# One weight load of a window-attention decode kernel, issued from ScalarE's DMA queue instead of SP's

## The chip, the cores and the metric

The kernel runs on one core of a Trainium2 chip. A core has a matrix engine (TensorE, PE in the profile), a vector engine (VectorE, DVE), an activation engine (ScalarE, ACT), a general engine (GpSimd, POOL) and a synchronization engine (SyncE, SP) that here only issues transfers. Each engine works through its own list of instructions in order and waits on semaphores that other engines or transfers raise. Transfers between device memory and the on-chip memory (128 partitions) run on 16 DMA engines. They are issued by an engine's instruction into that engine's queue: in the profile q1 is the queue of SP, q10 that of ScalarE.

The metric is the device time of one execution in microseconds, lower is better, as the median over runs. The profile is of one execution; its span is a little shorter than that execution's time.

## The reference, cut to what matters

```python
xn = layernorm(x)                                   # x: 2 x 1 x 512
# attention over the last W = 4096 of 32768 cached positions; 32 query heads, 8 kv heads, 128 wide
q = (xn @ wq).reshape(B, 1, 32, 128).transpose(0, 2, 1, 3)
k, v = (repeat(c[:, :, Sk - W:, :], 4, axis=1) for c in (k_cache, v_cache))
p = softmax(einsum("bhqd,bhkd->bhqk", q, k) * 128 ** -0.5)
s = einsum("bhqk,bhkd->bhqd", p, v).transpose(0, 2, 1, 3).reshape(B, 1, 4096) @ wo
# gated unit on the same xn; Fh = 896
z = gelu(xn @ w_in)                                 # w_in: 512 x 1792
z1, z2 = z[..., :Fh], layernorm(z[..., Fh:])
g = w_sp * z2 + b_sp                                # w_sp is 1 x 1, b_sp has one element
out = x + s * silu((z1 * g) @ w_out)                # w_out: 896 x 512
```

Everything is float32. For two rows of x the kernel reads 89.4 MB of weights and cache.

## The kernel before, in words

**The ring.** All large loads go into `ring` (line 80): four slots of 4 MB, 32 KB in each of the 128 partitions. `enqueue` (line 85) gives each load the next slot or slots in turn; `advance` (line 92) marks slots as free and issues whatever loads at the head of the list have all of theirs. The turn is fixed: w_in in slot 0 (3.5 MB), w_out in slot 1 (1.75 MB), wq in slots 2 and 3 (8 MB); then, for eight units (a unit is one batch row and two kv heads), k and v tiles of 4 MB in the order k0, k1, v0, k2, v1, k3 and so on, and last wo in seven pieces. The first three loads find their slots free and are issued at once, at lines 120 to 122; a later one is issued when its slot's last reader is done: k0 after the `z` matmuls (`advance(0)`), k1 after the `y` matmuls (`advance(1)`), v0 and k2 after the `q_ps` matmuls (`advance(2, 3)`), and from there a k tile's slot passes on after its last transpose, a v tile's after its `acc` matmuls. All these loads are issued by SP, in that order: a load that waits for its slot keeps those behind it waiting too.

**Order.** The engines TensorE, VectorE, ScalarE and SP are wrapped in `InOrder` (line 27), which keeps each one's instructions in the order of the program. Since its `issue` (line 37) emits them all, most rows of the profile name line 37; the tiles tell them apart.

**ScalarE's queue.** ScalarE issues three small loads: `xs` (x, 4 KB, line 109), then the two scalars of the gate, `w_sp` and `b_sp`, into `wb1` (lines 126 and 127; the profile calls the tile wb). Between line 109 and line 126 stand the three `enqueue` calls.

**The stages.** Layernorm of x gives `xnT`. TensorE computes `z` (xn @ w_in), and right behind it, as its next instruction, `wb_ps`, a small matmul that spreads the two scalars over the partitions:

```python
    advance(0)
    wb_ps = bank("wb_ps", "mo")[:, :2]
    pe.matmul(wb_ps, ones[0:1, :], wb1, start=True, stop=True)
    wb = const("wb", 2)
    dve.tensor_copy(wb, wb_ps)
    zs = const("zs", 2 * FQ)
    act.activation(zs, pz, AF.Copy)
```

On VectorE the copy into `wb` is followed by the transpose of `zs`, the gelu, the two means (matmuls `mean_ps` and `var_ps`) and `hT`. TensorE then does `y` (hT with w_out) and `yq`; VectorE and ScalarE make the sigmoid gate of it, which is used only at the very end. After `yq` TensorE does `q_ps` (xn @ wq); VectorE arranges q in `qbd`. Then the units follow: VectorE transposes each k tile in four pieces (`kt`, four a unit), TensorE multiplies (`sh`, `s`), softmax runs on VectorE and ScalarE, and TensorE applies v (`acc`) one unit behind. Last come the `part` and `so` matmuls with wo, the gate, the addition of x and the store.

Of the kernel before, what the change touches and what calls it, by code (L numbers as in the profile page):

```python
# [14 lines left out]
P = 128  # L15
# [27 lines left out]
def kernel(  # L43
# [14 lines left out]
    pe, dve, act, sp = (InOrder(tc, e) for e in (nc.tensor, nc.vector, nc.scalar, nc.sync))  # L58
# [7 lines left out]
    FT = FH // P  # L66
# [15 lines left out]
    queue = []  # L82
    turns = [0]

    def enqueue(load, count=1):

        at = turns[0] % 4
        turns[0] += count
        queue.append((load, range(at, at + count)))
        advance()  # L90

    def advance(*slots):
        for n in slots:
            free[n] = True
        while queue and all(free[n] for n in queue[0][1]):
            load, at = queue.pop(0)
            for n in at:
                free[n] = False
            load(ring[:, at[0] * SLOT : (at[-1] + 1) * SLOT], at[0])
# [9 lines left out]
    act.dma_start(xs, x[:, 0, :])  # L109
    weight = {}  # L110

    def load_rows(name, w, k):
        def load(t, at):
            n = k * w.shape[1]
            sp.dma_start(t[:, :n], w.rearrange("(p k) f -> p (k f)", p=P))
            weight[name] = t[:, :n].rearrange("p (k f) -> p k f", k=k)

        return load

    enqueue(load_rows("in", w_in, KT))  # L120
    enqueue(load_rows("out", w_out, FT))
    enqueue(load_rows("q", wq, KT), 2)
    win, wout, wqt = (weight[n] for n in ("in", "out", "q"))

# [391 lines left out]
    for n in range(EARLY):  # L516
        t, a = blocks[n]
# [5 lines left out]
    for n in range(EARLY, 32):  # L523
        if n == LATE:
            spread_quarters(so, parts, start=False, stop=False)
        t, a = blocks[n]
# [37 lines left out]
```

## Time and profile before

| what | value |
|---|---|
| median of 3 runs | 217.91 us (217.8 to 218.05) |
| the profiled execution's own time | 217.37 us |
| its span | 215.6 us |
| TensorE busy | 156.5 us, 73% |
| VectorE busy | 107.5 us, 50% |
| ScalarE busy | 44.0 us, 20% |
| large loads, on q1 | 89.40 MB, 97.0% of 16 DMA engines' time |
| granted TensorE clock, mean | 0.849 |

How to read the rows that follow. In a timeline a row is start, duration, engine, line, operation, output<-input, count, and in brackets the idle time before it and what ended that. In the chain that ended last, a row is start, duration and what the time went to. A row of the stages has the stage, its length, busy time and instructions of the five engines, the granted TensorE clock, the mean busy share of the DMA engines and GB/s. A DMA queue's row has packets, MB and the time of those packets as a share of 16 engines; packets are counted in the window in which they begin, so that a narrow window can show more than 100%. A DMA issue's row has the size and the time from issue to landing. A row of the waits has who waited for whom: us in total, times, longest.

### The profile page before, as it was taken

How to read it: one execution, taken by the hardware profiler on the slowest of the kernel's cores; microseconds unless marked ns; L12 is line 12 of the kernel's file. 1: busy time of each engine (PE TensorE's matmuls, PEld its weight loads, DVE VectorE, ACT ScalarE, POOL GpSimd, SP SyncE). 2: the span in 40 equal slices, each digit the busy share in tenths (PEclk: the TensorE clock that was granted, in tenths of full speed). 3: DMA queues.
4: the chain of work that ended last, by engine and by line, in shares of the span. 5: the costliest groups of instructions: out<-in, count | busy, mean ns of one | idle time of the engine just before them, and what ended most of it. 6: DMA issues, size and time to landing. Idle time of an engine off the chain costs nothing.

```text
span 215.6 us, 2230 instructions
## 1 busy us (share of the span) xinstructions
PE 156.5 (73%) x866; PEld 43.6 (20%) x866; DVE 107.5 (50%) x168; ACT 44.0 (20%) x109; POOL 3.9 (2%) x21
## 2 busy tenths in 40 slices
PE   0164273952994995995997699559959948999793
PEld 0121110210121221221221222222212212222321
DVE  3304313058968647837906941695587089240101
ACT  5002410000223143133113304120431421232001
POOL 6100000000000000000000000000000000000000
PEclk9999567695598899799699679958997995899799
DMA  7999898999999999999999999999999999999991
GB/s 251 426 528 401 389 499 371 423 444 409 456 407 450 426 435 432 426 438 413 450 412 438 432 438 435 432 432 407 432 444 423 444 426 450 413 441 413 404 388 40
DMA packets 3789, 89.54 MB, mean 415 GB/s; under 512 B 434, under 2 KB 450, under 8 KB 964
## 3 DMA queue, kind: packets, MB, share of 16 engines
q1 hardware_dynamic: 3772, 89.40, 97.0%
q8 instruction: 7, 0.11, 0.2%
q14 instruction: 2, 0.02, 0.0%
q10 hardware_dynamic: 8, 0.00, 0.0%
HBM read 89.40 MB, written 0.00 MB: 415 GB/s over the span
## 4 chain that ended last, share of the span: by engine, by line
DMA 48%; PE 34%; DVE 15%; issue 1%; SPq 0%; DVEq 0%
DMA ring<-in_A_wo_dram 20%; DMA ring<-in_A_wq_dram 16%; DMA ring<-in_A_k_cache_dram 12%; DVE kt L37 10%; PE s L37 10%; PE sh L37 9%; PE acc L37 7%; PE q_ps L37 4%; PE col L37 1%; PE mo L37 1%; DVE qm L37 1%; DVE qbd L37 1%; DVE m L37 1%; PE rp L37 1%; PE oT L37 0%
## 5 line engine op out<-in xcount | busy, mean ns | idle before, releaser
L37 DVE STREAM_TRANSPOSE kt<-ring 128x2048 f32<-128x2048 f32 x32 | 72.6, 2294 | 32.5 <-DMA ring<-in_A_k_cache_dram 30.5
L37 PE MATMUL sh<-kt,qbd 128*32 128x512 f32 x256 | 43.4, 727 | 14.0 <-DVE kt L37 14.0
L37 ACT ACTIVATE shs<-sh 128x512 f32<-128x512 f32 x32 | 19.1, 597 | 119.1 <-PE sh L37 119.1
L37 PE MATMUL s<-shs,add_dq 128*128 128x512 f32 x64 | 41.0, 748 | 0.0
L37 PE MATMUL acc<-ring,pT 128*32 128x512 f32 x256 | 30.3, 612 | 0.2 <-DVE pT L37 0.2
L37 PEld LDWEIGHTS s<-shs,add_dq 128*128 128x128 f32 x64 | 11.2, 219 | 31.1 <-issue 26.7
L37 PEld LDWEIGHTS sh<-kt,qbd 128*32 128x32 f32 x256 | 6.7, 114 | 34.2 <-issue 20.4
L37 PEld LDWEIGHTS acc<-ring,pT 128*32 128x32 f32 x256 | 7.4, 114 | 24.7 <-issue 15.5
L37 PE MATMUL q_ps<-ring,xnT 128*32 128x512 f32 x64 | 9.6, 770 | 3.6 <-DMA ring<-in_A_wq_dram 3.6
L37 PE MATMUL mo<-l,same_r 128*128 128x2 f32 x16 | 3.7, 299 | 10.7 <-ACT p L37 10.7
L37 DVE TENSOR_REDUCE m<-s 128x2 f32<-128x512 f32 x8 | 5.4, 675 | 9.1 <-PE s L37 9.1
L37 ACT ACTIVATE o<-acc,wd 128x128 f32<-128x128 f32 x32 | 9.1, 373 | 3.4 <-PE acc L37 3.4
L37 PE MATMUL z<-ring,xnT 128*32 128x448 f32 x32 | 5.6, 875 | 5.3 <-DMA ring<-in_B_w_in_dram 5.3
L37 ACT ACTIVATE p<-s,nb 128x256 f32<-128x256 f32 x16 | 7.6, 490 | 7.0 <-DVE nb L37 6.8
L37 PE MATMUL part<-ring,oT 128*32 128x512 f32 x56 | 7.9, 714 | 1.1 <-DMA ring<-in_A_wo_dram 1.1
L37 PE MATMUL col<-o,sel 128*32 128x512 f32 x16 | 8.3, 601 | 0.4 <-ACT o L37 0.4
L37 DVE STREAM_TRANSPOSE qT<-q_ps 128x512 f32<-128x512 f32 x2 | 1.4, 717 | 10.4 <-PE q_ps L37 10.2
L37 PE MATMUL y<-ring,hT 128*32 128x512 f32 x14 | 3.5, 1043 | 3.8 <-DVE hT L37 3.8
L37 DVE STREAM_TRANSPOSE pT<-p 128x512 f32<-128x512 f32 x8 | 5.4, 674 | 1.2 <-ACT p L37 1.2
L37 DVE TENSOR_TENSOR res<-so,gate 128x128 f32<-128x128 f32 x1 | 0.3, 292 | 10.8 <-PE so L37 10.8
L37 ACT ACT_TABLE_LOAD x4 | 5.1, 1283 | 1.9 <-issue 1.9
L37 PEld LDWEIGHTS mo<-l,same_r 128*128 128x128 f32 x16 | 3.0, 233 | 12.2 <-ACT p L37 12.2
(106 smaller groups left out, 63.2 us busy)
## 6 DMA issues: line engine op xcount, KB each, us to landing
ring<-in_A_k_cache_dram SPq DMA_DIRECT2D x8, 4096.0 KB, 27.5
ring<-in_A_v_cache_dram SPq DMA_DIRECT2D x8, 4096.0 KB, 30.1
ring<-in_A_wo_dram SPq DMA_DIRECT2D x1, 4096.0 KB, 34.2
ring<-in_B_w_in_dram SPq DMA_DIRECT2D x1, 3584.0 KB, 11.7
ring<-in_A_wo_dram SPq DMA_DIRECT2D x1, 2048.0 KB, 27.5
ring<-in_B_w_out_dram SPq DMA_DIRECT2D x1, 1792.0 KB, 15.5
ring<-in_A_wo_dram SPq DMA_DIRECT2D x1, 1024.0 KB
ring<-in_A_wo_dram SPq DMA_DIRECT2D x4, 256.0 KB, 16.7
```

The source lines that it names most:

```text
L37: return self.tc.keep_in_program_order(call(*args, **kwargs))
```

## The change

The helper that builds the loads of w_in, w_out and wq takes the issuing engine as an argument, SP unless another is given; for w_out ScalarE is given. The slots, the sizes, the access patterns and the order of the `enqueue` calls stay. In ScalarE's program the load stands where the `enqueue` call stands: behind `xs`, ahead of `w_sp` and `b_sp`. SP goes from w_in straight to wq.

```diff
-    def load_rows(name, w, k):
+    def load_rows(name, w, k, queue=sp):
         def load(t, at):
             n = k * w.shape[1]
-            sp.dma_start(t[:, :n], w.rearrange("(p k) f -> p (k f)", p=P))
+            queue.dma_start(t[:, :n], w.rearrange("(p k) f -> p (k f)", p=P))
             weight[name] = t[:, :n].rearrange("p (k f) -> p k f", k=k)
 
         return load
 
     enqueue(load_rows("in", w_in, KT))
-    enqueue(load_rows("out", w_out, FT))
+    enqueue(load_rows("out", w_out, FT, act))
     enqueue(load_rows("q", wq, KT), 2)
```

## The prediction

> **What bounds the kernel now.** I read the page first: busy shares, the slices, the DMA queues.
>
> ```profile
> span 215.6 us, 2230 instructions
> ...
> DMA  7999898999999999999999999999999999999991
> ...
> q1 hardware_dynamic: 3772, 89.40, 97.0%
> q8 instruction: 7, 0.11, 0.2%
> ...
> q10 hardware_dynamic: 8, 0.00, 0.0%
> ```
>
> q1 is SP's queue, with every large load; q10 is ScalarE's, with eight tiny packets. q1 keeps the 16 DMA engines busy for 97% of the span. To see whether that stream ever breaks I asked for busy time by stage, for VectorE's waits, and for the chain that ended last.
>
> ```profile
> 10.00:36.00 26.00, 11.08 (x60) 3.61 (x60) 6.66 (x26) 4.65 (x8) 0.00 (x0) 0.77 1.01 437
> 36.00:212.00 176.00, 144.46 (x798) 39.39 (x802) 96.45 (x122) 36.42 (x97) 0.00 (x0) 0.85 0.99 425
> ...
> DVE kt L37 <- DMA ring<-in_A_k_cache_dram: 30.5, 5, 7.4
> ...
> 1.65 34.42 DMA ring<-in_A_wq_dram
> 36.11 9.70 PE q_ps L37 x64
> ...
> 201.94 9.95 DMA ring<-in_A_wo_dram
> ```
>
> The last columns are the DMA share and GB/s: 1.01 and 0.99 from 10 to 212 us. Between those, compute alternates with the stream, and five times VectorE sits waiting for a k tile, up to 7.4 us. So the end is set by 89 MB through a queue that must not run dry, plus the 4 us around it. Moving a transfer within the stream costs nothing by itself; a load issued after the stream has caught up with it costs the whole gap. The question is what the change does to the issue times of the k and v loads.
>
> **The change, part by part.** The issues as they stand, from the timelines of SP and ScalarE (start, duration):
>
> ```profile
> 0.73 0.40 SPq L37 DMA_DIRECT2D ring<-in_B_w_in_dram  x1
> 1.20 0.41 SPq L37 DMA_DIRECT2D ring<-in_B_w_out_dram  x1
> 1.65 0.46 SPq L37 DMA_DIRECT2D ring<-in_A_wq_dram  x1
> ...
> 0.73 0.54 ACTq L37 DMA_DIRECT2D xs<-in_A_x_dram  x1
> 1.31 0.23 ACTq L37 DMA_DIRECT2D wb<-in_B_w_sp_dram  x1
> 1.57 0.27 ACTq L37 DMA_DIRECT2D wb<-in_B_b_sp_dram  x1
> ```
>
> SP loses one issue of 0.41 us, so wq is issued at 1.20 instead of 1.65; it stands behind w_in's rows either way, worth 0. ScalarE gains an issue of 0.41 us at 1.31, between xs and the two scalars, which go out at about 1.7 and 2.0; xs stays ahead of them all, and the layernorm behind xs ends well before w_in lands, so this too is 0. The count of DMAs does not change.
>
> What does change is the order on the DMA engines. How the engines share two queues is visible from q10's packets, found by asking for the DMA traffic in narrow windows: 0 to 2.5 us; 2.5 to 5.7; 5.8 to 5.9; 7.3 to 8.3; 9.0 to 9.1; then 17 to 34 us for wq.
>
> ```profile
> q10 hardware_dynamic: 4, 0.00, 1.3%
> ...
> q1 hardware_dynamic: 36, 1.03, 76.2%
> ...
> q10 hardware_dynamic: 1, 0.00, 0.6%
> ...
> q1 hardware_dynamic: 16, 0.46, 106.2%
> q10 hardware_dynamic: 1, 0.00, 0.1%
> ...
> q10 hardware_dynamic: 1, 0.00, 0.6%
> ...
> q1 hardware_dynamic: 112, 7.34, 99.6%
> ```
>
> The first four are xs and its completion marks. Then q10 moves nothing until 5.85 us, although w_sp was issued at 1.31; and the last of the scalars' four packets (w_sp, its mark, b_sp, its mark) comes at 9.05, the others one per us between. A w_in row (28 KB) takes 1.06 us: sixteen in one us on sixteen engines at 106%. So 4 packets of 4 bytes spanned three w_in rows: the engine gives each queue one packet in turn, and a mark is a packet. Of wq, 112 packets in 17 us at 99.6% of 16 engines make 64 KB and 2.42 us each. Each engine holds eight rows of each load; a w_out row is half a w_in row, 0.53 us (estimate from its bytes), a k or v row half a wq row, 1.21.
>
> The Trainium skill, "DMA: Bandwidth & Descriptors", section "Queues, rings and completion order", says that each engine goes round its queues packet by packet, and that a packet often holds 9 to 17 descriptors. The first half agrees with the four packets above; by the second, w_out's eight rows would pass in one turn, which is the second rival.
>
> Step 1: w_in. w_out now takes the place that w_sp had in ScalarE's queue, so I put its first row on that engine at 5.85, after three w_in rows. The five that remain alternate with five w_out rows: w_in lands 5 x 0.53 = 2.65 us later. The rows of today, with the landing of w_in:
>
> ```profile
> ring<-in_B_w_in_dram SPq DMA_DIRECT2D x1, 3584.0 KB, 11.7
> ...
> 12.56 5.61 PE L37 MATMUL z<-ring,xnT 128*32 128x448 f32 x32 [5.33 <-DMA ring<-in_B_w_in_dram]
> ...
> 18.10 0.38 PE L37 MATMUL wb_ps<-wb,ones 1*128 1x2 f32 x2
> ...
> 27.77 3.55 PE L37 MATMUL y<-ring,hT 128*32 128x512 f32 x14 [3.84 <-DVE hT L37]
> 32.03 0.42 PE L37 MATMUL yq<-ys,rowm 128*32 128x128 f32 x8 [0.71 <-ACT ys L37]
> ```
>
> z goes from 12.56 to 15.2 and ends at 20.8; k0, released by z's end, is issued at 20.9, while wq's rows last until 36: hidden. With nothing else late, y would end at 34.0, yq at 35.1, and the q matmuls could still start at 36.11.
>
> Step 2: the two scalars. They are behind w_out's eight rows, and their four packets take turns with wq's rows. On their engine, from 5.85: five pairs to 13.8; w_out's sixth row, w_in's mark, w_out's seventh to 14.9; a wq row to 17.3, the eighth row to 17.8, wq to 20.2, w_out's mark, wq to 22.7, w_sp, wq to 25.1, its mark, wq to 27.5, b_sp, wq to 29.9, b_sp's mark. With 0.3 us to land and wake, wb_ps starts at 30.2 or 30.3 instead of 18.10: 12.2 us later. Queued behind that wait on TensorE are the mean and variance matmuls, y, yq and all of q; on VectorE the copy of wb stands ahead of the transpose that starts the gelu; on SP, k1 waits for y's end, with v0 and k2 behind it. One turn earlier or later for the first w_out row moves this by one wq row, 2.4 us; bounds from one turn to five give 25.5 to 35.1.
>
> Step 3: what hangs on it. y needs w_out, whose last row passes at 17.8: no wait. The chain from wb_ps to yq's end lasted 14.35 us (18.10 to 32.45), so q's matmuls go from 36.11 to 44.6: 8.5 us. k1's issue was at y's end, 13.28 after wb_ps.
>
> ```profile
> 31.38 0.55 SPq L37 DMA_DIRECT2D ring<-in_A_k_cache_dram  x1
> 42.39 0.54 SPq L37 DMA_DIRECT2D ring<-in_A_v_cache_dram  x1
> 73.79 0.54 SPq L37 DMA_DIRECT2D ring<-in_A_k_cache_dram  x1
> ...
> ring<-in_A_k_cache_dram SPq DMA_DIRECT2D x1, 4096.0 KB, 28.3
> ...
> 95.16 2.31 DVE L37 STREAM_TRANSPOSE kt<-ring 128x2048 f32<-128x2048 f32 x1 [4.27 <-DMA ring<-in_A_k_cache_dram]
> ```
>
> k1 goes from 31.38 to 43.6. k0 was issued at 18.23 and landed 28.3 us later, at 46.5, and in the stream k1 follows to 56.2 (8 rows, 9.7 us). What does an issue into an almost empty queue take? The nearest row is w_in at the start: 11.7 us from issue to landing for 8 x 1.06 = 8.5 us of rows, so 3.2 us besides. For k1: 43.6 + 3.2 + 9.7 = 56.5, or 0.3 later than the stream. The lower bound is 0 (k0's last rows cover it), the upper 3.2 (nothing does). I add 0.5 because landing is set by the engine that is furthest behind: the seven instruction fetches take 0.2% of 16 x 215.6 us, 1.0 us each of one engine, so engines are up to 1 us apart, and those ahead lose their lead in a dry spell, then meet the later fetches (0 to 1.0; the middle).
>
> k3's issue hangs on q by compute alone: 73.79 + 8.5 = 82.3, landing 82.3 + 12.9 = 95.2 against 95.1 now and 95.4 with the shift: just in time, 0 more (a little slower compute makes it 0.5). v0, k2 and v1 have over 3 us to spare: v0 at 42.39 + 8.5 = 50.9 against 56.5 less 3.2, the others later still against a stream 9.7 us a tile. After k3 the delay goes into waits that exist: VectorE waited 4.27 us for k3 and up to 7.4 for later tiles, 30.5 in all, so from k5 on nothing is late but the stream.
>
> Sum: 0.3 + 0.5 = +0.8 us. The profiled execution took 217.37 us (215.6 of span); its own would be 218.2. It stands 0.54 below the median of 217.91, so against the median I say 218.7. About 0.2%, 0.4 us, is what a measurement of this kernel can tell.
>
> **The rivals.** First, later turns: the first w_out row one turn later, since w_out's issue is longer than w_sp's (0.41 against 0.23 us) and meets wq's. wb_ps at 32.7, k1 at 46.0, landing 58.9: 2.7 + 0.5 = +3.2, at most 221.1; two turns, 223.5. For it: w_sp's descriptor waited 4.5 us for its turn, for a reason the trace does not show.
>
> Second, all hidden, 217.9. Either w_out comes after one or two w_in rows, wb_ps at 25.5 or 27.9 and k1 at 38.8 or 41.2, over 2 us before it is needed; or its rows pass in one turn, 8 x 0.53 = 4.2 us, so that w_in lands at 16.7 and the scalars directly behind, at about 11; yq then ends at 36.7, q starts 0.6 late, and the stream notices nothing. Against the one turn: w_sp's mark did not pass with w_sp.
>
> The Trainium skill, same page, section "Rules for kernel authors", holds that spreading loads over issuing engines gives no bandwidth and saves only issue time. That rule gives this rival's time, and names no cost for what shares the queue.
>
> Third, faster: the start. From 0 to 10 us the stream has not its full rate:
>
> ```profile
> 2.00:3.00 1.00, 0.00 (x0) 0.00 (x0) 0.62 (x2) 1.00 (x1) 1.00 (x4) 1.00 0.43 143
> 3.00:4.00 1.00, 0.00 (x0) 0.00 (x0) 0.37 (x3) 0.66 (x3) 0.87 (x5) 1.00 0.83 344
> ```
>
> Rows of a second queue could fill these two us: at 430 GB/s they would move 0.37 MB more, 0.9 us of stream, if w_out's rows are served from 2.3 us. That gives 217.0 to 217.4 if k1 is in time. Against it: q10 was not served in 2.5 to 5.7.
>
> **How the numbers follow.** Just late, as summed: 0.42, own range 218.1 to 219.4, of it 0.06 inside 0.2%. Later turns: 0.22. Hidden: 0.25. Faster: 0.11. Slower is 0.36 + 0.22 = 0.58, the same 0.06 + 0.25 = 0.31, faster 0.11. The range leaves out two turns' delay and the lower part of the faster case: 217.4 to 221.2.
>
> **What would show it.** Step 1: z's first matmul near 15.2. Step 2: wb_ps 25 to 33 us in, TensorE idle for some 9 us after z until the wb load lands; that is the step I would give up first. Step 3: k1 issued near 43.6, q's matmuls right behind yq near 44.6, GB/s falling for a moment around 45, and VectorE's wait for k3 gone. The forecast is wrong if wb_ps starts before 22, if DMA share stays at 1 around 45 and the time moves all the same, or if w_in comes no later.

## The result and the profile after

The changed kernel takes 218.85 us (218.62 to 219.36) against 217.91 us (217.65 to 218.37; six executions of each): 1.0046 times the time before, with a 95% interval of 1.0035 to 1.0058. It is slower by 0.94 us; the forecast was 218.7. The profiled execution took 218.89 us, with a span of 216.9; that of before was 0.54 us below its median, so the two profiled executions differ by 1.5 us, and their spans by 1.3, where the medians differ by 0.94. Differences of time below are between medians; what is read from the two profiles has to be set against 1.3.

From the page of the changed kernel:

```profile
span 216.9 us, 2230 instructions
...
GB/s 257 423 487 429 399 544 314 465 308 456 413 441 423 435 435 432 435 423 441 417 446 405 459 411 447 414 447 423 447 423 426 429 435 429 417 444 417 407 373 34
...
q1 hardware_dynamic: 3628, 87.57, 94.5%
q10 hardware_dynamic: 152, 1.84, 2.0%
```

w_out's 1.84 MB have moved to q10. The ninth slice, 43 to 49 us, has only 308 GB/s; single slices vary, since a packet counts where it begins, so wider and better placed windows follow. From its chain that ended last (start, duration, what) and its waits in the first 46 us (who for whom: total, times, longest):

```profile
2.02 28.17 DMA wb<-in_B_b_sp_dram
...
PE wb_ps L37 <- DMA wb<-in_B_b_sp_dram: 9.8, 1, 9.8
...
SPq L37 <- PE y L37: 22.3, 1, 22.3
```

A load of four bytes heads the chain: 28 us from its issue to its landing. TensorE waits 9.8 us for it, and SP stands 22.3 us in front of k1, until `y` is done. The stages on TensorE, and k1's issue:

```profile
15.16 5.32 PE L37 MATMUL z<-ring,xnT 128*32 128x448 f32 x32 [7.63 <-DMA ring<-in_B_w_in_dram]
30.33 0.55 PE L37 MATMUL wb_ps<-wb,ones 1*128 1x2 f32 x2 [9.84 <-DMA wb<-in_B_b_sp_dram]
...
39.94 3.59 PE L37 MATMUL y<-ring,hT 128*32 128x512 f32 x14 [3.84 <-DVE hT L37]
44.24 0.43 PE L37 MATMUL yq<-ys,rowm 128*32 128x128 f32 x8 [0.71 <-ACT ys L37]
44.49 7.05 PE L37 MATMUL q_ps<-ring,xnT 128*32 128x512 f32 x64
...
43.59 0.55 SPq L37 DMA_DIRECT2D ring<-in_A_k_cache_dram  x1
```

The forecast had z at 15.2, wb_ps at 30.2 to 30.3, k1 at 43.6, q's matmuls at 44.6. The stages around k1's issue (the last two columns are DMA share and GB/s), first the changed kernel, then the one before; the last row of each covers six us:

```profile
10.00:36.00 26.00, 6.95 (x38) 2.97 (x38) 3.16 (x13) 2.05 (x3) 0.00 (x0) 0.75 1.01 437
...
42.00:44.00 2.00, 1.53 (x6) 0.00 (x0) 0.00 (x0) 0.41 (x1) 0.00 (x0) 0.66 0.83 360
44.00:46.00 2.00, 1.75 (x24) 0.77 (x28) 0.85 (x3) 0.50 (x2) 0.00 (x0) 1.00 0.83 262
46.00:48.00 2.00, 2.00 (x24) 0.60 (x20) 0.91 (x2) 0.00 (x0) 0.00 (x0) 1.00 0.95 410
...
44.00:50.00 6.00, 5.75 (x60) 1.94 (x64) 1.76 (x4) 0.50 (x2) 0.00 (x0) 1.00 0.88 347
```

```profile
44.00:46.00 2.00, 1.75 (x20) 0.24 (x8) 0.89 (x2) 0.00 (x0) 0.00 (x0) 1.00 1.14 492
...
44.00:50.00 6.00, 2.87 (x22) 0.67 (x10) 3.55 (x12) 0.00 (x0) 0.00 (x0) 0.85 1.01 437
```

From 10 to 36 us the stream runs at 437 GB/s, as before: two queues do not slow it. The rows of two us swing (262 after, 492 before, in the same stage), because a packet counts where it begins. Over the six us from 44 to 50 the changed kernel moves 347 GB/s and the kernel before 437: 6 x (437 - 347) / 437 = 1.24 us of stream are missing, and the spans of these two profiles differ by 1.3. The time was lost there. The end of k1 says the same: the last of its sixteen completion marks begins at 55.76 us before the change and at 56.68 after it, 0.9 us later.

How it was lost, from q1's rows of the changed kernel at 44.0 to 44.9 and at 44.9 to 46 us:

```profile
q1 hardware_dynamic: 16, 0.00, 1.0%
...
q1 hardware_dynamic: 16, 0.52, 149.7%
```

In the first window only k0's sixteen marks begin, one on each engine, and no row. In the second the first sixteen rows of k1 begin, the earliest at 44.94, 1.35 us after k1's issue. They take 1.65 us on average (149.7% of 16 engines for 1.1 us, over 16 rows), where the prediction's estimate for a k row was 1.21 and the rows behind them do take 1.21. So the engines first stand still and then start slowly.

The order of packets behind it, from q10's rows in narrow windows of the changed kernel: 2.5 to 5.4 us (no q10 row, so nothing), 13 to 15, 16.8 to 17.7, 19.7 to 20.6, and 22 to 23, 24.5 to 25.5, 27 to 28, 29.5 to 30.5 (the first row is q1's, from 2.5 to 5.4):

```profile
q1 hardware_dynamic: 33, 0.95, 76.5%
...
q10 hardware_dynamic: 32, 0.46, 53.5%
...
q10 hardware_dynamic: 16, 0.23, 59.4%
...
q10 hardware_dynamic: 16, 0.00, 1.0%
...
q10 hardware_dynamic: 1, 0.00, 0.1%
q10 hardware_dynamic: 1, 0.00, 0.1%
q10 hardware_dynamic: 1, 0.00, 0.1%
q10 hardware_dynamic: 1, 0.00, 0.1%
```

Until 5.4 us w_out is not served. From 13 to 15 its sixth and seventh rows pass on all 16 engines, near 17 the eighth, near 20 the 16 marks, and then one small packet every 2.4 us: w_sp, its mark, b_sp, its mark, one wq row between each two.

### The profile page after: what moved, and what is told of

It is laid out like the page before. It is cut to its first block, busy times and chain, and to the rows that moved or that the text cites. A ratio compares the mean times of both kernels' runs of the same rounds, so it can differ in the third digit from the quotient of the medians.

```text
span 216.9 us, 2230 instructions
## 1 busy us (share of the span) xinstructions
PE 152.4 (70%) x866; PEld 44.0 (20%) x866; DVE 107.6 (50%) x168; ACT 44.0 (20%) x109; POOL 3.9 (2%) x21
## 3 DMA queue, kind: packets, MB, share of 16 engines
q10 hardware_dynamic: 152, 1.84, 2.0%
## 4 chain that ended last, share of the span: by engine, by line
PE 45%; DMA 31%; DVE 18%; issue 2%; ACT 1%; ACTq 1%; DVEq 0%
PE sh L37 13%; PE s L37 13%; DMA wb<-in_B_b_sp_dram 13%; DVE kt L37 11%; DMA ring<-in_A_k_cache_dram 11%; PE acc L37 8%; DMA ring<-in_A_wo_dram 7%; PE q_ps L37 3%; PE y L37 2%; PE col L37 2%; PE mo L37 1%; DVE u L37 1%; DVE qm L37 1%; DVE qbd L37 1%; DVE m L37 1%
## 5 line engine op out<-in xcount | busy, mean ns | idle before, releaser
L37 DVE STREAM_TRANSPOSE kt<-ring 128x2048 f32<-128x2048 f32 x32 | 72.3, 2291 | 17.7 <-DMA ring<-in_A_k_cache_dram 17.7
L37 PE MATMUL sh<-kt,qbd 128*32 128x512 f32 x256 | 45.6, 734 | 11.3 <-DVE kt L37 11.3
L37 PE MATMUL s<-shs,add_dq 128*128 128x512 f32 x64 | 40.2, 735 | 0.0
L37 PE MATMUL acc<-ring,pT 128*32 128x512 f32 x256 | 29.8, 604 | 0.2 <-DVE pT L37 0.2
L37 PEld LDWEIGHTS sh<-kt,qbd 128*32 128x32 f32 x256 | 7.3, 117 | 30.6 <-issue 16.6
L37 PE MATMUL wb_ps<-wb,ones 1*128 1x2 f32 x2 | 0.6, 343 | 9.8 <-DMA wb<-in_B_b_sp_dram 9.8
L37 PE MATMUL q_ps<-ring,xnT 128*32 128x512 f32 x64 | 7.0, 592 | 0.0
```

The costliest lines, as they stand in the source:

```text
L37: return self.tc.keep_in_program_order(call(*args, **kwargs))
```

## The experiments

**The scalars first.** w_out stays on ScalarE's queue; only its place among that queue's loads is changed.

```diff
+    wb1 = cst.tile([1, 2], F32, tag="wb1", name="wb1")
+    act.dma_start(wb1[:, 0:1], ...w_sp...)
+    act.dma_start(wb1[:, 1:2], ...b_sp...)
     enqueue(load_rows("in", w_in, KT))
     enqueue(load_rows("out", w_out, FT, act))
     enqueue(load_rows("q", wq, KT), 2)
-
-    wb1 = cst.tile([1, 2], F32, tag="wb1", name="wb1")
-    act.dma_start(wb1[:, 0:1], ...w_sp...)
-    act.dma_start(wb1[:, 1:2], ...b_sp...)
```

> w_out stays on ScalarE's queue; the loads of w_sp and b_sp are issued ahead of it. Theory (the time was lost because the two scalars waited behind w_out, so that k1 was issued at 43.6 us, into a queue about to run dry): two queues share the engines as before, so w_in still lands some 2.65 us late and z starts near 15.2, but the scalars land near 9 and wb_ps follows z at about 20.5; on the scalars' engine w_out's last row and mark pass only near 30, just when y wants it; k1 is issued near 34, the stream never stops, time 217.9 (217.6 to 218.3). Rival 1 (the second queue itself costs: the engines lose time by switching, or w_in's delay of 2.65 us is paid at the end): 218.8, as with the change. Rival 2 (the start fills better with two queues): 217.0 to 217.4.

Measured: 218.14 us against 218.04 (the kernel before, on the same chip in the same series), 1.0001 times (0.9991 to 1.0011). TensorE's timeline, and k1's issue:

```profile
15.66 5.91 PE L37 MATMUL z<-ring,xnT 128*32 128x448 f32 x32 [8.29 <-DMA ring<-in_B_w_in_dram]
21.50 0.38 PE L37 MATMUL wb_ps<-wb,ones 1*128 1x2 f32 x2
...
34.87 0.55 SPq L37 DMA_DIRECT2D ring<-in_A_k_cache_dram  x1
...
40.00:50.00 10.00, 3.74 (x34) 0.96 (x24) 6.69 (x16) 0.00 (x0) 0.00 (x0) 0.92 0.97 418
```

The second queue is there, z is 3.1 us later than before, and nothing is lost: from 40 to 50 us the stream runs at 418 GB/s, against 421 before and 365 with the change. Some steps came later than expected, z by 0.5 us, wb_ps by 1.0 and k1's issue by 0.9, for reasons that were not looked into; k1 was still in time. So the second queue and w_in's delay cost nothing that can be told, 0.2 us at most (1.0011): the cost of the change is the place of the two scalars behind w_out. A gain of more than 0.1% at the start is excluded too.

**The scalars' wait alone.** No large load leaves SP's queue; the two scalars move onto it, behind wq.

```diff
-    act.dma_start(wb1[:, 0:1], ...w_sp...)
-    act.dma_start(wb1[:, 1:2], ...b_sp...)
+    sp.dma_start(wb1[:, 0:1], ...w_sp...)
+    sp.dma_start(wb1[:, 1:2], ...b_sp...)
```

> All large loads on SP's queue as before the change, and the two scalars on it too, behind wq: the wait for the scalars alone, with no second queue beside the loads. Theory: the scalars land with wq, near 36.1; wb_ps starts near 36.3, y ends and k1 is issued 13.26 us later, at 49.6, which is 6.0 later than with the change; the queue has been dry since 44 to 46 us, so each of these 6 us is lost: 218.85 + 6.0 = 224.8 (223.5 to 225.5), with the DMA share near 0 for some 5 us before 51. Rival 1 (the second queue costs, not the scalars' wait): 217.9. Rival 2 (a late k1 is partly caught up, because the stream is not what sets the end): between 218.9 and 222.

Measured: 224.31 us, 1.0292 times (1.0275 to 1.0309). Its timelines of TensorE and SP, and the stages around the gap:

```profile
35.60 0.55 PE L37 MATMUL wb_ps<-wb,ones 1*128 1x2 f32 x2 [17.76 <-DMA wb<-in_B_b_sp_dram]
...
48.51 0.55 SPq L37 DMA_DIRECT2D ring<-in_A_k_cache_dram  x1
...
42.00:44.00 2.00, 0.00 (x0) 0.00 (x0) 0.36 (x3) 1.51 (x3) 0.00 (x0) 0.50 0.80 344
44.00:46.00 2.00, 0.79 (x4) 0.20 (x8) 0.94 (x5) 0.00 (x0) 0.00 (x0) 0.50 0.00 0
46.00:48.00 2.00, 2.00 (x14) 0.38 (x6) 0.00 (x0) 0.00 (x0) 0.00 (x0) 0.52 0.00 0
48.00:50.00 2.00, 1.29 (x19) 0.51 (x20) 0.29 (x1) 0.61 (x2) 0.00 (x0) 1.00 0.40 115
```

k0's last rows, begun before 44 us, end by 44.9; then nothing moves until k1's first row begins at 49.85, 1.34 us behind its issue. With one queue for all loads a longer wait for the same two scalars, 17.8 us on TensorE instead of 9.8, costs 6.3 us. wb_ps came 0.7 us sooner than expected, probably because the scalars' packets end with one DMA engine's share of wq, and wq's landing is that of the last of sixteen; k1 was issued at 48.5, not 49.6, and the time was 224.3 us, not 224.8.

**w_out as two loads.** Same bytes, twice as many packets ahead of the scalars.

```diff
-            queue.dma_start(t[:, :n], w.rearrange("(p k) f -> p (k f)", p=P))
+            src = w.rearrange("(p k) f -> p (k f)", p=P)
+            at = [0, 4 * w.shape[1], n] if name == "out" else [0, n]
+            for a, b in zip(at, at[1:]):
+                queue.dma_start(t[:, a:b], src[:, a:b])
```

> As the change, but w_out is issued as two loads, of four and three of its seven blocks: rows of 8 and 6 KB, sixteen and two marks on each engine ahead of the scalars instead of eight and one. Same bytes. Theory (the engine gives each queue one packet in turn, so that each further packet ahead of the scalars costs one packet of SP's queue): w_in lands about 1.1 us sooner than with the change, z starts near 14.1; w_out itself and the scalars last through all of wq and into k0, b_sp's mark passes near 42.1; wb_ps near 42.4, k1 near 55.7, 12.1 us later than with the change, time 231 (229 to 232.5). Rival 1 (the queues share by bytes): the scalars land as with the change, near 30, time 218.8. Rival 2 (a load passes as a whole in a turn): scalars near 11, time 217.9.

Measured: 231.36 us, 1.0610 times (1.0595 to 1.0625). TensorE and SP:

```profile
14.07 5.07 PE L37 MATMUL z<-ring,xnT 128*32 128x448 f32 x32 [5.86 <-DMA ring<-in_B_w_in_dram]
42.74 0.55 PE L37 MATMUL wb_ps<-wb,ones 1*128 1x2 f32 x2 [23.59 <-DMA wb<-in_B_b_sp_dram]
...
55.84 0.55 SPq L37 DMA_DIRECT2D ring<-in_A_k_cache_dram  x1
```

Every step is within 0.4 us of the turn-by-turn count (14.1, 42.4, 55.7, 231). Sharing by bytes would have left the scalars at 30 us, and a load that passes whole would have freed them at 11; both fall. The Trainium skill, "DMA: Bandwidth & Descriptors", section "Queues, rings and completion order", says that an engine switches queues only between packets: the runs agree, with wb_ps at 42.74 us where counting by turns gave 42.4. It calls 9 to 17 descriptors to a packet typical; here each row and each mark took a turn of its own.

**wq as two loads.** With the change, but each turn of SP's queue half as long.

```diff
-            queue.dma_start(t[:, :n], w.rearrange("(p k) f -> p (k f)", p=P))
+            src = w.rearrange("(p k) f -> p (k f)", p=P)
+            at = [0, n // 2, n] if name == "q" else [0, n]
+            for a, b in zip(at, at[1:]):
+                queue.dma_start(t[:, a:b], src[:, a:b])
```

> As the change, but wq is issued as two loads, one for each of its two slots: rows of 32 KB instead of 64 KB, so that a turn of SP's queue takes 1.21 us instead of 2.42. Same bytes. Theory (packet by packet): w_in and z as with the change (z near 15.2); from 13.8 us on, the scalars' engine passes w_out's last three rows, its mark and the scalars' four packets against six turns of 1.21 us: b_sp's mark near 22.7, wb_ps near 23.0, k1 near 36.3, long before the stream needs it: 217.9 (217.6 to 218.3). Rival 1 (sharing by bytes, or the scalars wait for something else than the turns): wb_ps near 30.3 and 218.8. Rival 2 (the second queue itself costs): wb_ps near 23, and still 218.8.

Measured: 218.56 us against 218.04, 1.0025 times (1.0012 to 1.0037).

```profile
15.24 5.61 PE L37 MATMUL z<-ring,xnT 128*32 128x448 f32 x32 [7.48 <-DMA ring<-in_B_w_in_dram]
23.15 0.35 PE L37 MATMUL wb_ps<-wb,ones 1*128 1x2 f32 x2 [2.31 <-DMA wb<-in_B_b_sp_dram]
...
36.26 0.55 SPq L37 DMA_DIRECT2D ring<-in_A_k_cache_dram  x1
...
40.00:50.00 10.00, 6.67 (x58) 1.72 (x50) 3.75 (x13) 0.00 (x0) 0.00 (x0) 0.97 0.99 424
```

The place of wb_ps (23.0 expected) and of k1 (36.3) came out, and with half-length turns the scalars are back in time: the stream has no gap from 40 to 50 us (DMA share 0.99). But the run was 0.5 us slower than before, against an expected 0 and outside the range expected for the mechanism. So the same split of wq was also run on one queue, and the same kernel again:

> The kernel before, all large loads on SP's queue, only wq issued as two loads, one for each slot. It asks whence the 0.5 us come that the change with wq in two loads still lost (218.56 against 218.04), although k1 was issued in time. Theory A (one more load, and wq in smaller rows, costs by itself, or moves the clock's phases at the end): 218.4 to 218.7 here too. Theory B (a second queue beside SP's costs 0.5 us when nothing waits for it): 217.9 to 218.2 here, and the repeated run of the other kernel again near 218.5; but then the run with the scalars first, which has the second queue too, should not have been at 218.1.

> The change with wq in two loads once more, on another chip or at another hour. If its 0.5 us are a property of the kernel: 218.5 to 218.6, with the stream unbroken until 210 us and the difference behind it, in how late TensorE ends the last matmuls. If they were an accident of the first series: 217.9 to 218.2.

Measured, against 218.10 for the kernel before: 218.44 with one queue, 1.0015 times (1.0004 to 1.0026); 218.21 in the repeat, 1.0007 (0.9997 to 1.0017). So the split goes with some 0.3 us without any second queue (at most 0.6, by the interval), and the two-queue kernel did not repeat its 0.5. The chain that ended last of the one-queue run ends otherwise than before the change:

```profile
202.19 8.95 PE part L37 x56
...
211.22 0.60 ACT parts L37
...
211.87 0.91 PE so L37 x24
```

There the last matmuls with wo, not the landing of wo's last piece, set the end. Why they do in some executions was not tried, and the 0.5 us stay open.

## Why the prediction was right

The forecast was +0.8 us by one mechanism, and the runs show that mechanism and exclude the rivals. By its steps:

- **What bounds the kernel.** The queue that must not run dry: over the runs k1's issue at 34.87 us cost nothing (at 36.26, with wq split, 0.1 to 0.5), at 43.59 0.94 us, at 48.51 6.27, at 55.84 13.32. Subtracting the cost from the issue gives 42.65, 42.24 and 42.52: k1 is needed at about 42.5 us, and every microsecond later is lost in full, to within 0.4 us over these three runs. The prediction's own limit was 43.6 - 0.8 = 42.8. The trace gives it a third way: k0's marks begin at 44.10 us in the changed kernel and k1's first row 1.35 us after its issue, so that an issue after some 42.75 us leaves engines without work.
- **Issue times on SP and ScalarE worth 0.** Not tested by themselves; the run with the scalars first bounds them, with all else but the scalars' wait, at 0.2 us (1.0011).
- **Step 1, w_in 2.65 us later.** z moved by 2.60, and that is hidden: right.
- **Step 2, the scalars' turns.** wb_ps at 30.33 against 30.2 to 30.3. The step I had offered to give up first held: taking w_sp's old turn for w_out's first was right, although why the first turn comes only after three w_in rows is still not shown. The 0.3 us to land and wake, for which the prediction showed no row, were 0.55: b_sp's mark begins at 29.78.
- **Step 3, k1 at 43.6 and its price.** The issue was right (43.59). The price was made of 0.3 and 0.5, chosen inside bounds of 0 to 3.2 and 0 to 1.0; that their sum came as near to 0.94 as 0.8 is in part luck. The 0.94 was not split into the two terms, but the traces bear out the mechanism of the second: before the change k0's marks were spread over 1.9 us (44.12 to 46.04), and an instruction fetch of 1.0 us on one engine fell among its rows, at 40.9; in the changed kernel they are spread over 0.65 us (44.10 to 44.75), the fetch comes behind the gap, at 49.2, and k1's last mark is 1.1 us behind the one before it. The slow first rows of k1, 1.65 us instead of 1.21, were not counted by themselves; they lie in the 3.2 us that the prediction took from w_in.
- **Step 3, k3 "just in time".** Mis-sized. k3 was to be issued at 82.3 and was at 79.43, mostly because q's matmuls took 7.05 us instead of 9.64. So k3 had more to spare than the sum said. VectorE's wait for k3 is gone, as forecast, and its waits for k tiles fell from 30.5 to 17.7 us:

```profile
DVE kt L37 <- DMA ring<-in_A_k_cache_dram: 17.7, 4, 6.4
```

- **The rivals.** A turn later (+3.2) did not come. "All hidden" is what happens once the scalars are ahead of w_out. "Faster" falls: with two queues and the scalars first the ratio was 1.0001.

## What to carry to other kernels

Before a large load is moved to another queue, list the small loads behind it there and who waits for them. In these runs a DMA engine with two queues to serve charged a four-byte load one full row of the other queue (2.42 us beside wq) for every packet ahead of it, its own and the bulk load's completion marks included. Where a stream of loads is the bound, read each load's issue time against the time at which the stream needs it; here a delay was free up to that time and cost its whole length beyond it. Put tiny loads first, or keep bulk loads off their queue.

## What the runs showed of the hardware that was not expected

q's 64 matmuls took 9.64 us when TensorE had stood idle for 3.65 us before them, and 7.05 us when they followed `yq` at once; the granted clock was 0.50 from 36 to 40 us before the change, and 1.00 from 44 to 48 after it. The late start thus gave back 2.6 us of compute, off the path that sets the end. Following `yq` at once is not enough by itself: in the run with wq in two loads q's matmuls did so too, from 37.35 us, and took 8.66 us at a granted clock of 0.50 until 40 us. Their time goes with the granted clock while they run; what sets its phases was not tried. First the kernel before, then the changed one, then wq in two loads:

```profile
36.00:40.00 4.00, 3.89 (x20) 0.97 (x24) 0.00 (x0) 0.00 (x0) 0.00 (x0) 0.50 1.00 434
...
36.11 9.64 PE L37 MATMUL q_ps<-ring,xnT 128*32 128x512 f32 x64 [3.65 <-DMA ring<-in_A_wq_dram]
```

```profile
44.00:48.00 4.00, 3.75 (x44) 1.36 (x48) 1.76 (x4) 0.50 (x2) 0.00 (x0) 1.00 0.89 336
```

```profile
36.00:40.00 4.00, 3.29 (x27) 1.08 (x28) 1.76 (x4) 0.91 (x2) 0.00 (x0) 0.50 1.06 459
...
37.35 8.66 PE L37 MATMUL q_ps<-ring,xnT 128*32 128x512 f32 x64
```
